# Weight splits of the second routed expert placed among the routing operations, with new planner durations for the routed blocks

## Chip, cores and metric

One core of one Trainium2 chip runs the whole program. The metric is the device time of one execution in microseconds (us); lower is better. The time before is the median of three executions.

## The reference

Three layers run one after the other: attention over a window of 64 tokens (2 batches, 8 heads, 576 tokens, head size 64), a dense mixture of 4 experts, and a routed mixture of 8 experts. 1152 tokens of 512 numbers pass through the last two. The part that matters here is the last:

```python
def _moe2_ref(x, w_skip, w_gate, w1, w2):
    do_compute = x @ w_skip > 0
    xc = x[do_compute]
    logits = xc @ w_gate
    e_idx = np.argmax(logits, axis=1)
    probs = softmax(logits); gate_w = probs[range(len(xc)), e_idx]
    for e in range(8):
        mask = e_idx == e
        h = np.maximum(xc[mask] @ w1[e], 0.0)
        y[mask] = gate_w[mask, None] * (h @ w2[e])
    out[do_compute] = xc + y
```

Each token goes to one expert or to none. w1 is 512 by 1024 and w2 is 1024 by 512 for each expert.

## The kernel before, in words

**Arithmetic.** Every fp32 operand of a large product is written as a high and a low part, and a product is three TensorE (PE) products: high by high, low by high, high by low. For weights, ScalarE (ACT) casts a loaded piece of 128 by 1024 to the high part (`hi` in `w_split`, L348), and VectorE (DVE) subtracts it to get the low part (`lo`, L351): the "split". A routed expert has two weight passes (w1 and w2, `w_pass` L1057) of four pieces each, so eight casts and eight splits. The tiles are `wa1h`, `wa1l`, `wa2h`, `wa2l` and the same with `wb`: two sets that alternate from expert to expert. Expert 0 uses wb, expert 1 wa, expert 6 wb, expert 7 wa.

**A routed block** (`block`, L948) is 128 tokens of one expert, gathered by index. First product g1 (24 PE instructions, 12 for each half of the hidden size); ACT's `hr` (relu, L989) for each half; four PE transposes `pt<-ident,hr` for each half (`turn`, L1006); ACT's and DVE's `ht` high and low (L1010, L1013); second product g2; DVE's `xg` (L1049) adds the gated result, and POOL's `scatter` (L910) writes the rows out. Within block e the tokens of block e+1 are transposed (`xpose`, L381) and split (`xsplit`, ACT L941 and DVE L943, tile `xs`), and the weights of expert e+1 are cast and split. The transposes of hr, xg, hr, xg use a ring of two PSUM buffers in turn, so the transposes of the second `hr` overwrite what DVE's first `ht` has to have read.

**Routing** (`route`, L668) runs for nine token tiles, between the last tiles of the dense layer. For each tile DVE finds the best expert (`top`, `early`) and the token's rank, PE sums into a table `tab`; `idx` (L843) makes the gather indices `idg` out of it, `num` (L853) the counts `cnt`. `gates` (L799, operations L777 to L783) splits the last two tiles' gate values in small bf16 pieces; `spread` (L785, `wy`) and PE's `tab<-wy` (L794) put them in the table, and `rest` (L867) reads them back. The first routed block takes its tokens by rank (`grab`, L760), not by index.

**What sets the order.** A small planner (`Plan`, L109) takes operations with an engine, a duration that is a formula of the size (`c_act`, `c_dve`), what they read and write, and a priority. It lists them in the order of its own simulated start, and the engines execute that static order. An operation of ACT or DVE with priority 0 or more may not start in the plan if it would delay a waiting one of negative priority by more than a margin. One plan covers the dense layer's end, routing and block 0; then there is one plan for each expert's block. After each plan but the last stands `tails` (L1175), an `If` on the counts with further blocks for experts with over 128 tokens. What an engine first has to wait for behind such an `If` it waits for as of that engine's end of the stretch before.

Of the kernel before, what the change touches and what calls it, by code (L numbers as in the profile page):

```python
# [13 lines left out]
ALU = mybir.AluOpType  # L14
# [7 lines left out]
FF = 1024  # L22
E1 = 4
E2 = 8
# [197 lines left out]

@with_exitstack
def fused_kernel(ctx: ExitStack, tc: tile.TileContext, q, k, v, dp, w1, w2, wskip, wgate, m1, m2, out):
# [116 lines left out]
    def w_split(b, ring, key, part, c, prio, pool=False, after=(), hpool=False, hdve=False):  # L341
        def aps():
            h, l = ring[f"{part}h"], ring[f"{part}l"]
            if part == 1:
                return h[:, c, :], l[:, c, :]
            return tuple(x[:, 2 * c:2 * c + 2, :].rearrange("p a n -> p (a n)") for x in (h, l))

        def hi():  # L348
            (POOL.tensor_copy if hpool else DVE.tensor_copy if hdve else ACT.copy)(out=aps()[0], in_=b.tile)  # L349

        def lo():  # L351
            h, l = aps()
            (POOL if pool else DVE).tensor_tensor(out=l, in0=b.tile, in1=f32(h), op=ALU.subtract)  # L353

        add("POOL" if hpool else "DVE" if hdve else "ACT", 3.5 if hpool else c_dve(FF // 2) if hdve else c_act(FF, False), hi, rd=[b], wr=[(key, part, "h", c)], prio=prio)
        if pool:
            add("POOL", 2.3, lo, rd=[b, (key, part, "h", c)], wr=[(key, part, "l", c)], prio=prio)
        else:
            add("DVE", c_dve(FF), lo, rd=[b, (key, part, "h", c), *after], wr=[(key, part, "l", c)], prio=prio)
        b.close()  # L360
# [307 lines left out]
    def route(t):  # L668
# [66 lines left out]
        add("DVE", 0.35, early, rd=[K("oh"), K("m8"), o0], wr=[o1, K("w0"), K("mm")], prio=P)  # L735
# [67 lines left out]
        def weigh(after):  # L803
            add("DVE", 0.8, slot, rd=[K("ps"), *after], wr=[K("r"), K("oj")], prio=1)
            if t < TT - 2:
                gates()
                spread(0, 5, 2)
            else:
                spread(0, 2, 1)
                later.append(lambda: (gates(["idg", ("htl", 4)], 15), spread(2, 5, 15, ["idg"])))  # L810
# [5 lines left out]
        if t == GT:  # L816
            add("DVE", 0.35, id0, rd=[("tab", 0), ("tab", 1)], wr=["id0"], prio=2)
# [22 lines left out]
    def route_end():  # L840
# [8 lines left out]
        add("DVE", 0.45, idx, rd=[("tab", 0), ("tab", 1)], wr=["idg"], prio=-1)  # L849
# [83 lines left out]
    def xsplit(ps, pr, n=128):  # L933

        x, w = M["xs"].buf(), KC // len(ps)
        for i, p in enumerate(ps):
# [4 lines left out]
            add("ACT", c_act(n * w), lambda v=v, hi=hi: ACT.copy(out=hi(), in_=v()), rd=[p, "M"] + ([x] if i else []),  # L941
                wr=[(x, "h", k) for k in ks], new=None if i else [x], prio=pr)
            add("DVE", c_dve(n * w), lambda v=v, hi=hi, lo=lo: DVE.tensor_tensor(out=lo(), in0=v(), in1=f32(hi()), op=ALU.subtract),  # L943
# [4 lines left out]
    def block(e, j, xg, x, small=False, amid=None):  # L948
# [29 lines left out]
        def g1(c0, w):  # L978
# [10 lines left out]
            add("ACT", c_act(128 * w), lambda: ACT.activation(out=hr[:, 0:128 * w], in_=ps[:, 0:128 * w],  # L989
# [5 lines left out]
        def tr(c0, w, hr):  # L995
# [14 lines left out]
            add("ACT", c_act(w * n), lambda: ACT.activation(out=ht[:, s, 0:n], in_=p[:, 0:w, 0:n],  # L1010
                                                            func=ACTF.Relu if small else ACTF.Copy),
                rd=[p], wr=[(ht, "h", c0)], new=[ht] if c0 == 0 else None, prio=-1)
            add("DVE", c_dve(w * n), lambda: DVE.scalar_tensor_tensor(  # L1013
# [42 lines left out]

    def w_pass(kd, e, p, prio=None):  # L1057
# [5 lines left out]
        for c in range(4):  # L1063
            extra = kd == "r" and e > 0 and p == 2
            st = KN["w2s"] if (kd, e, p) == ("m", 0, 2) else 2.5
            b = w_load(src, p, c, prio + st * c, extra, early=kd == "r" and e > 2 and p == 1)
            w_split(b, ring, key, p, c, prio + st * c, pool=(kd, e, p) == ("m", 0, 2) and KN["w2pool"][c],
                    after=["idg"] if kd == "r" and e == 1 else [])

    with tc.manual_schedule():  # L1070
# [138 lines left out]
        for e in range(E2):  # L1209
            if e < E2 - 2:  # L1210
# [5 lines left out]
            block(e, 0, xgs[e, 0], xts[e, 0], amid=None if e else route_gates)  # L1216
            if e == 0:
# [47 lines left out]
```

## Time and profile before

| | |
|---|---|
| median of 3 executions | 644.83 us (644.16 to 646.07) |
| profiled execution | 646.72 us, of which the span from first to last instruction is 644.8 us |
| PE busy | 623.1 us, 97% of the span |
| DVE, ACT, POOL busy | 52%, 36%, 12% |
| mean DMA rate | 114 GB/s |
| dense layer and routing end, block 0 begins | 482.93 us |
| blocks 1, 2, 3, 4, 5, 6, 7 begin | 498.89, 525.66, 549.21, 562.57, 598.21, 611.46, 625.30 us |
| last DVE operation and last scatter | about 639.7 and 639.98 us |

Experts 1, 2 and 4 had further blocks within their `tails`; behind experts 0, 3, 5 and 6 the next full block follows at once. Times in a timeline are microseconds from the start of the span. A time in brackets behind a row is how long the engine had been idle before it, and after the arrow what ended that wait. A letter q behind an engine's name is its sequencer, which runs the branches.

### The profile page before, as it was taken

To read this page: it belongs to the slowest core of one execution; us is meant where nothing else is said; L and a number is where in the kernel's file an instruction comes from. 1 tells how busy PE (TensorE), PEld (TensorE's weight loads), DVE (VectorE), ACT (ScalarE), POOL (GpSimd) and SP (SyncE) were. 2 spreads that over 40 slices of the span, in tenths; PEclk is the share of its full clock that TensorE was granted. 3 is DMA by queue.
4 is the path that set the end of the run, shared out by engine and by line. 5 is a ranking of instruction groups with operands and counts; after the bars stand their busy time and mean duration, and the time that the engine had idled before them with its cause. 6 is when DMAs were issued, how large, how long until landed. Compare 5 with 4: busy or idle time off the path is not lost. (4 is left out here: it accounts for less than half of the span.)

```text
span 644.8 us, 9918 instructions
## 1 busy us (share of the span) xinstructions
PE 623.1 (97%) x3742; PEld 545.3 (85%) x3742; DVE 338.5 (52%) x757; ACT 230.6 (36%) x484; POOL 76.2 (12%) x103
## 2 busy tenths in 40 slices
PE   8799999999999999999999999999998999999986
PEld 7688898998989899898989898979886778788865
DVE  5888731226612115421213526888868846872881
ACT  5668730114401113310103320202344654762761
POOL 3222320000000000000000000000104422330320
PEclk9999999999999999999999999999999999999998
DMA  9893119934700002500000511015277968692630
GB/s 222 196 286 101 35 2 2 7 12 149 243 1 0 2 1 82 179 0 1 1 0 3 197 63 72 28 66 164 80 247 236 332 214 320 214 376 76 208 132 10
DMA packets 60512, 73.49 MB, mean 114 GB/s; under 512 B 37105, under 2 KB 37105, under 8 KB 60440
## 3 DMA queue, kind: packets, MB, share of 16 engines
q1 hardware_dynamic: 57736, 64.55, 37.2%
q0 software_dynamic: 2704, 8.02, 4.0%
q8 instruction: 41, 0.67, 0.5%
q14 instruction: 31, 0.25, 0.2%
HBM read 65.85 MB, written 7.49 MB: 114 GB/s over the span
## 5 line engine op out<-in xcount | busy, mean ns | idle before, releaser
L542 PE MATMUL mm<-xth,wa1h 128*128 128x384 f32 (+1 forms) x416 | 136.9, 329 | 0.0
L542 PE MATMUL mm<-xtl,wa1h 128*128 128x384 f32 (+1 forms) x416 | 135.7, 326 | 0.0
L542 PE MATMUL mm<-xth,wa1l 128*128 128x384 f32 (+1 forms) x416 | 135.7, 326 | 0.0
L548 ACT ACTIVATE hh<-mm 128x384 fp32r<-128x384 f32 (+1 forms) x104 | 48.5, 466 | 239.6 <-PE mm L542 234.0
L563 PE MATMUL mm<-wa2h,hh 128*128 128x512 f32 (+1 forms) x296 | 117.0, 395 | 0.0
L550 DVE SCALAR_TENSOR_TENSOR hl<-mm,hh 128x384 fp32r<-128x384 f32 (+1 forms) x104 | 54.8, 527 | 117.9 <-ACT hh L548 117.3
L563 PE MATMUL mm<-wa2h,hl 128*128 128x512 f32 (+1 forms) x296 | 115.0, 389 | 0.0
L563 PE MATMUL mm<-wa2l,hh 128*128 128x512 f32 (+1 forms) x296 | 114.9, 388 | 0.0
L542 PEld LDWEIGHTS mm<-xth,wa1h 128*128 128x128 f32 x416 | 78.7, 189 | 0.7 <-issue 0.2
L542 PEld LDWEIGHTS mm<-xtl,wa1h 128*128 128x128 f32 x416 | 78.7, 189 | 0.5
L542 PEld LDWEIGHTS mm<-xth,wa1l 128*128 128x128 f32 x416 | 78.8, 189 | 0.0
L563 PEld LDWEIGHTS mm<-wa2h,hl 128*128 128x128 f32 x296 | 55.7, 188 | 12.4
L563 PEld LDWEIGHTS mm<-wa2h,hh 128*128 128x128 f32 x296 | 55.8, 188 | 11.4
L563 PEld LDWEIGHTS mm<-wa2l,hh 128*128 128x128 f32 x296 | 55.8, 188 | 11.2
L575 DVE SCALAR_TENSOR_TENSOR x<-mm,prob,x 128x512 f32<-128x512 f32 (+1 forms) x28 | 20.5, 732 | 76.2 <-PE mm L563 75.9
L818 POOL DMA_INDIRECT x<-scr,id x1 | 2.0, 1970 | 370.5 <-DMA scr<-x 370.5
L353 DVE TENSOR_TENSOR wa2l<-raw,wa2h 128x1024 fp32r<-128x1024 f32 x32 | 39.1, 1233 | 5.0 <-ACT wa2h L349 4.9
L349 ACT CAST wa2h<-raw 128x1024 fp32r<-128x1024 f32 x32 | 33.3, 1050 | 23.1 <-PE mm L563 18.6
L353 DVE TENSOR_TENSOR wa1l<-raw,wa1h 128x1024 fp32r<-128x1024 f32 x32 | 38.2, 1228 | 4.8 <-PE mm L965 3.0
L349 ACT CAST wa1h<-raw 128x1024 fp32r<-128x1024 f32 x32 | 32.0, 1046 | 16.8 <-DMA raw<-in_moe_w_dram 8.3
L1013 DVE SCALAR_TENSOR_TENSOR ht<-pt,ht 128x512 fp32r<-128x512 f32 (+2 forms) x27 | 15.1, 568 | 29.8 <-ACT ht L1010 27.5
L463 POOL TENSOR_TENSOR s<-s,mx 128x512 f32<-128x512 f32 x18 | 18.8, 1048 | 57.8 <-DVE mx L460 39.7
(212 smaller groups left out, 896.1 us busy)
## 6 DMA issues: line engine op xcount, KB each, us to landing
raw<-in_moe_w_dram SPq DMA_DIRECT2D x96, 512.0 KB
scr<-x SPq DMA_DIRECT2D x9, 256.0 KB
out_dram<-x SPq DMA_DIRECT2D x9, 256.0 KB
qn<-in_q_dram SPq DMA_DIRECT2D x8, 256.0 KB
kn<-in_k_dram SPq DMA_DIRECT2D x8, 256.0 KB
vn<-in_v_dram SPq DMA_DIRECT2D x8, 256.0 KB
raw<-wgt SPq DMA_DIRECT2D x4, 512.0 KB
qn<-in_q_dram SPq DMA_DIRECT2D x2, 128.0 KB
```

The source lines that it names most:

```text
L349: (POOL.tensor_copy if hpool else DVE.tensor_copy if hdve else ACT.copy)(out=aps()[0], in_=b.tile)
L353: (POOL if pool else DVE).tensor_tensor(out=l, in0=b.tile, in1=f32(h), op=ALU.subtract)
L463: add("POOL", 1.0, lambda: POOL.tensor_tensor(out=s.tile, in0=s.tile, in1=mx[:, 3].unsqueeze(2).to_broadcast([128, HP, 128]), op=ALU.mult) ...
L542: PE.matmul(out=ps[:, 0:n], lhsT=wa[a][:, kk, f * 128:(f + 1) * 128], rhs=x[:, kk, g0:g0 + n], start=(i == 0), stop=(i == 3 * KC - 1))
L548: add("ACT", c_act(n), lambda: ACT.activation(out=hh[:, f, 0:n], in_=ps[:, 0:n], func=ACTF.Relu), rd=[ps], wr=[("hh", f)], prio=-1)
L550: add("DVE", c_dve(n), lambda: DVE.scalar_tensor_tensor(out=hl[:, f, 0:n], in0=ps[:, 0:n], scalar=0.0, in1=f32(hh[:, f, 0:n]), op0=ALU.max ...
L563: PE.matmul(out=ps[:, 0:c1 - c0], lhsT=x[:, f, o:o + 128], rhs=wa[a][:, f, c0:c1], start=(f == 0 and i == 0), stop=(f == FC - 1 and i == 2))
L575: DVE.scalar_tensor_tensor(out=z, in0=y, scalar=prob[:, t, e:e + 1], in1=z, op0=ALU.mult, op1=ALU.add)
L818: add("POOL", 1.0, lambda: POOL.indirect_dma_start(out=R["x0"], out_offset=None, in_=scr[0:128 * (GT + 1), :], in_offset=bass.IndirectOffs ...
L1013: add("DVE", c_dve(w * n), lambda: DVE.scalar_tensor_tensor(out=ht[:, s, n:2 * n], in0=p[:, 0:w, 0:n], scalar=0.0, in1=f32(ht[:, s, 0:n]), ...
```

## The change

There are five edits. (1) `r_act` and `r_dve` are the old duration formulas plus 0.1 and 0.08 us; the planner now uses them for `hr`, `ht`, `xs` and for the casts and splits of all routed weights. (2) The four w1 splits of expert 1 no longer wait for `idg` all together. `first_lows` gives the first piece a dependence on the routing step `early` of tile 6; the second and third piece are cut in two halves of 512 columns, which depend on the last but one tile's rank matmul, on `cnt` (two of them) and on `idg`; the fourth depends on `idg`. (3) `gates` no longer depends on the low part of block 0's second `ht`. (4) `id0`, the indices of the first gather, has priority -1 in place of 2, and `idx` counts 0.7 in place of 0.45. (5) The gather for expert 0's third block is declared behind block 0 instead of ahead of it. DVE has two instructions more, since two splits became four halves.

```diff
--- before.py
+++ after.py
@@ -220,6 +220,14 @@
 
+def r_act(n, psum=True):
+    return c_act(n, psum) + 0.1
+
+
+def r_dve(n):
+    return c_dve(n) + 0.08
+
+
 @with_exitstack
@@ -338,7 +346,7 @@
 
-    def w_split(b, ring, key, part, c, prio, pool=False, after=(), hpool=False, hdve=False):
+    def w_split(b, ring, key, part, c, prio, pool=False, after=(), hpool=False, hdve=False, ca=c_act, cd=c_dve, lows=None):
         def aps():
@@ -348,15 +356,17 @@
 
-        def lo():
+        def lo(s=slice(0, FF)):
             h, l = aps()
-            (POOL if pool else DVE).tensor_tensor(out=l, in0=b.tile, in1=f32(h), op=ALU.subtract)
-
-        add("POOL" if hpool else "DVE" if hdve else "ACT", 3.5 if hpool else c_dve(FF // 2) if hdve else c_act(FF, False), hi, rd=[b], wr=[(key, part, "h", c)], prio=prio)
+            (POOL if pool else DVE).tensor_tensor(out=l[:, s], in0=b.tile[:, s], in1=f32(h)[:, s], op=ALU.subtract)
+
+        add("POOL" if hpool else "DVE" if hdve else "ACT", 3.5 if hpool else c_dve(FF // 2) if hdve else ca(FF, False), hi, rd=[b], wr=[(key, part, "h", c)], prio=prio)
         if pool:
...
         else:
-            add("DVE", c_dve(FF), lo, rd=[b, (key, part, "h", c), *after], wr=[(key, part, "l", c)], prio=prio)
+            for s, w in lows or ((slice(0, FF), after),):
+                add("DVE", cd(s.stop - s.start), lambda s=s: lo(s), rd=[b, (key, part, "h", c), *w],
+                    wr=[(key, part, "l", c)], prio=prio)
         b.close()
@@ -732,7 +742,7 @@
 
-        add("DVE", 0.35, early, rd=[K("oh"), K("m8"), o0], wr=[o1, K("w0"), K("mm")], prio=P)
+        add("DVE", 0.35, early, rd=[K("oh"), K("m8"), o0], wr=[o1, K("w0"), K("mm"), ("early", t)], prio=P)
         add("ACT", 0.24, lambda: ACT.activation(out=T("ex"), in_=src()[:, 0:E2], func=ACTF.Exp,
@@ -807,14 +817,14 @@
                 spread(0, 2, 1)
-                later.append(lambda: (gates(["idg", ("htl", 4)], 15), spread(2, 5, 15, ["idg"])))
+                later.append(lambda: (gates(["idg"], 15), spread(2, 5, 15, ["idg"])))
 
...
         if t == GT:
-            add("DVE", 0.35, id0, rd=[("tab", 0), ("tab", 1)], wr=["id0"], prio=2)
+            add("DVE", 0.35, id0, rd=[("tab", 0), ("tab", 1)], wr=["id0"], prio=-1)
             add("POOL", 1.0, lambda: POOL.indirect_dma_start(
@@ -846,7 +856,7 @@
 
-        add("DVE", 0.45, idx, rd=[("tab", 0), ("tab", 1)], wr=["idg"], prio=-1)
+        add("DVE", 0.7, idx, rd=[("tab", 0), ("tab", 1)], wr=["idg"], prio=-1)
         add("PE", 0.03, lambda: PE.matmul(out=R["pf"][:, 0:E2], lhsT=R["ones"], rhs=R[o], start=True, stop=True),
@@ -938,9 +948,9 @@
             lo = lambda i=i: x[:, i * w:(i + 1) * w, 0:n, 1]
-            add("ACT", c_act(n * w), lambda v=v, hi=hi: ACT.copy(out=hi(), in_=v()), rd=[p, "M"] + ([x] if i else []),
+            add("ACT", r_act(n * w), lambda v=v, hi=hi: ACT.copy(out=hi(), in_=v()), rd=[p, "M"] + ([x] if i else []),
                 wr=[(x, "h", k) for k in ks], new=None if i else [x], prio=pr)
-            add("DVE", c_dve(n * w), lambda v=v, hi=hi, lo=lo: DVE.tensor_tensor(out=lo(), in0=v(), in1=f32(hi()), op=ALU.subtract),
+            add("DVE", r_dve(n * w), lambda v=v, hi=hi, lo=lo: DVE.tensor_tensor(out=lo(), in0=v(), in1=f32(hi()), op=ALU.subtract),
                 rd=[p, x] + [(x, "h", k) for k in ks], wr=[(x, "l", k) for k in ks], prio=pr)
@@ -986,7 +996,7 @@
             gemm(f"g1{c0}", ps, 1, parts)
-            add("ACT", c_act(128 * w), lambda: ACT.activation(out=hr[:, 0:128 * w], in_=ps[:, 0:128 * w],
+            add("ACT", r_act(128 * w), lambda: ACT.activation(out=hr[:, 0:128 * w], in_=ps[:, 0:128 * w],
                                                               func=ACTF.Copy if small else ACTF.Relu),
@@ -1007,10 +1017,10 @@
             hr.close()
-            add("ACT", c_act(w * n), lambda: ACT.activation(out=ht[:, s, 0:n], in_=p[:, 0:w, 0:n],
+            add("ACT", r_act(w * n), lambda: ACT.activation(out=ht[:, s, 0:n], in_=p[:, 0:w, 0:n],
                                                             func=ACTF.Relu if small else ACTF.Copy),
                 rd=[p], wr=[(ht, "h", c0)], new=[ht] if c0 == 0 else None, prio=-1)
-            add("DVE", c_dve(w * n), lambda: DVE.scalar_tensor_tensor(
+            add("DVE", r_dve(w * n), lambda: DVE.scalar_tensor_tensor(
                 out=ht[:, s, n:2 * n], in0=p[:, 0:w, 0:n], scalar=0.0, in1=f32(ht[:, s, 0:n]), op0=ALU.max,
@@ -1054,6 +1064,11 @@
 
+    first_lows = [[(slice(0, FF), [("early", TT - 3)])],
+                  [(slice(0, FF // 2), [("r", "ps", (TT - 2) % 2)]), (slice(FF // 2, FF), ["cnt"])],
+                  [(slice(0, FF // 2), ["cnt"]), (slice(FF // 2, FF), ["idg"])],
+                  [(slice(0, FF), ["idg"])]]
+
     def w_pass(kd, e, p, prio=None):
@@ -1065,7 +1080,9 @@
             w_split(b, ring, key, p, c, prio + st * c, pool=(kd, e, p) == ("m", 0, 2) and KN["w2pool"][c],
-                    after=["idg"] if kd == "r" and e == 1 else [])
+                    after=["idg"] if kd == "r" and e == 1 else [],
+                    lows=first_lows[c] if (kd, e, p) == ("r", 1, 1) else None,
+                    **(dict(ca=r_act, cd=r_dve) if kd == "r" else {}))
 
@@ -1207,13 +1224,15 @@
         for e in range(E2):
-            if e < E2 - 2:
+            if 0 < e < E2 - 2:
                 xgs[e, 2] = gather(e, 2, 7, [("g2", 0)])
...
             block(e, 0, xgs[e, 0], xts[e, 0], amid=None if e else route_gates)
+            if e == 0:
+                xgs[e, 2] = gather(e, 2, 7, [("g2", 0)])
             if e == 0:
```

**DVE, block 0,** from the indices to the second half of the block as it was. `ht` is the low part of a half of the hidden layer, `wa1l` and `wa2l` are expert 1's splits.

```order
L847 TENSOR_SCALAR idg<-a 128x72
L353 TENSOR_TENSOR wa1l<-raw,wa1h 128x1024
L1013 SCALAR_TENSOR_TENSOR ht<-pt,ht 128x4x128
L353 TENSOR_TENSOR wa1l<-raw,wa1h 128x1024 x2
L1013 SCALAR_TENSOR_TENSOR ht<-pt,ht 128x4x128
L353 TENSOR_TENSOR wa1l<-raw,wa1h 128x1024
L777 TENSOR_SCALAR sc_1361<-sc_1361 128x1
...
L789 TENSOR_TENSOR wy_1356<-w_1354,oj_1350 128x216
L353 TENSOR_TENSOR wa2l<-raw_4238,wa2h 128x1024
L353 TENSOR_TENSOR wa2l<-raw_4254,wa2h 128x1024
L943 TENSOR_TENSOR xs_4417<-pt,xs_4417 128x512
```

DVE at the same place in the change:

```order
L361 TENSOR_TENSOR wa1l<-raw,wa1h 128x512 x2
L855 TENSOR_SCALAR tb<-tab 128x9x8
...
L857 TENSOR_SCALAR idg<-a 128x72
L1023 SCALAR_TENSOR_TENSOR ht<-pt,ht 128x4x128
L787 TENSOR_SCALAR sc_1361<-sc_1361 128x1
...
L799 TENSOR_TENSOR wy_1356<-w_1354,oj_1350 128x216
L1023 SCALAR_TENSOR_TENSOR ht<-pt,ht 128x4x128
L361 TENSOR_TENSOR wa1l<-raw,wa1h 128x512
L361 TENSOR_TENSOR wa1l<-raw,wa1h 128x1024
L953 TENSOR_TENSOR xs_4415<-pt,xs_4415 128x512
```

The first `wa1l` and three of the four halves are now ahead of `idg` (two halves are the fence's first row); only a half and a whole are left behind it. They stand behind `wy` and the second `ht`, and the gates follow the first `ht` directly. All four `wa2l` come behind the block's `xg` (before: two ahead of it, two behind).

**DVE, block 6,** whose weights are expert 7's, as it was; a first `wa1l` stands ahead of the two shown. The blocks 2 to 5 show the same pattern.

```order
L353 TENSOR_TENSOR wa1l<-raw,wa1h 128x1024 x2
L1013 SCALAR_TENSOR_TENSOR ht<-pt,ht 128x4x128
L353 TENSOR_TENSOR wa1l<-raw,wa1h 128x1024
L353 TENSOR_TENSOR wa2l<-raw_7318,wa2h 128x1024
L943 TENSOR_TENSOR xs_7397<-pt,xs_7397 128x512
L1013 SCALAR_TENSOR_TENSOR ht<-pt,ht 128x4x128
L353 TENSOR_TENSOR wa2l<-raw_7327,wa2h 128x1024
L943 TENSOR_TENSOR xs_7422<-pt,xs_7422 128x512
L353 TENSOR_TENSOR wa2l<-raw_7352,wa2h 128x1024
L1049 SCALAR_TENSOR_TENSOR xg<-mm,gates,xg 128x512
L353 TENSOR_TENSOR wa2l<-raw_7367,wa2h 128x1024
L1177 COMPARE_AND_BRANCH
```

DVE in block 6 in the change, again behind a first `wa1l`:

```order
L361 TENSOR_TENSOR wa1l<-raw,wa1h 128x1024 x2
L1023 SCALAR_TENSOR_TENSOR ht<-pt,ht 128x4x128
L953 TENSOR_TENSOR xs_7395<-pt,xs_7395 128x512
L1023 SCALAR_TENSOR_TENSOR ht<-pt,ht 128x4x128
L361 TENSOR_TENSOR wa1l<-raw,wa1h 128x1024
L953 TENSOR_TENSOR xs_7419<-pt,xs_7419 128x512
L361 TENSOR_TENSOR wa2l<-raw_7320,wa2h 128x1024
L1059 SCALAR_TENSOR_TENSOR xg<-mm,gates,xg 128x512
L361 TENSOR_TENSOR wa2l<-raw_7329,wa2h 128x1024
L361 TENSOR_TENSOR wa2l<-raw_7353,wa2h 128x1024
L361 TENSOR_TENSOR wa2l<-raw_7362,wa2h 128x1024
L1194 COMPARE_AND_BRANCH
```

Both list all eight splits of the next expert. Before, seven stand ahead of `xg` and one behind it. After, five stand ahead and three behind.

**PE, block 5,** around the transposes of the first half of the hidden layer, as it was; blocks 1 to 6 show the same.

```order
L965 MATMUL mm<-wa1h,xs_6440 128x512
L965 MATMUL mm<-wa1l,xs_6440 128x512
L1006 MATMUL pt<-ident,hr 128x128 x4
L965 MATMUL mm<-wa1h,xs_6440 128x512
L965 MATMUL mm<-wa1l,xs_6440 128x512
L965 MATMUL mm<-wa1h,xs_6440 128x512
L965 MATMUL mm<-wa1l,xs_6440 128x512
L965 MATMUL mm<-wa1h,xs_6440 128x512 x4
L965 MATMUL mm<-wa2h,ht 128x512
```

PE at the same place in the change:

```order
L975 MATMUL mm<-wa1h,xs_6437 128x512
L975 MATMUL mm<-wa1l,xs_6437 128x512
L975 MATMUL mm<-wa1h,xs_6437 128x512
L975 MATMUL mm<-wa1l,xs_6437 128x512
L975 MATMUL mm<-wa1h,xs_6437 128x512
L975 MATMUL mm<-wa1l,xs_6437 128x512
L1016 MATMUL pt<-ident,hr 128x128 x4
L975 MATMUL mm<-wa1h,xs_6437 128x512 x4
L975 MATMUL mm<-wa2h,ht 128x512
```

The transposes `pt<-ident,hr` stand behind 20 of the 24 g1 instructions, not behind 16, so that four instead of eight lie between them and the first g2 instruction, which reads `ht`.

## Rows read from the trace of the kernel before

**Rows 1.** The page's busy time: us, share of the span, instructions.

```profile
PE 623.1 (97%) x3742; PEld 545.3 (85%) x3742; DVE 338.5 (52%) x757; ACT 230.6 (36%) x484; POOL 76.2 (12%) x103
```

**Rows 2.** PE's waits from 440 to 645: us in total, times, longest.

```profile
PE mm L965 <- DVEq L1177: 1.9, 1, 1.9
PE tab L794 <- DVE gb L780: 1.5, 1, 1.5
```

**Rows 3.** DVE's timeline, block 0 and start of block 1: start, us, operation.

```profile
486.70 0.20 DVE L847 TENSOR_SCALAR idg<-a 128x72 uint32<-128x72 f32 x1
486.81 1.22 DVE L353 TENSOR_TENSOR wa1l<-raw,wa1h 128x1024 fp32r<-128x1024 f32 x1
488.95 0.69 DVE L1013 SCALAR_TENSOR_TENSOR ht<-pt,ht 128x512 fp32r<-128x512 f32 x1 [0.92 <-ACT ht L1010]
489.56 2.35 DVE L353 TENSOR_TENSOR wa1l<-raw,wa1h 128x1024 fp32r<-128x1024 f32 x2
...
495.90 0.67 DVE L789 TENSOR_TENSOR wy<-w,oj 128x216 bf16<-128x216 bf16 x2
...
501.19 2.35 DVE L353 TENSOR_TENSOR wa2l<-raw,wa2h 128x1024 fp32r<-128x1024 f32 x2
```

**Rows 4.** PE's timeline of the same stretch, with its waits.

```profile
490.10 0.33 PE L1006 MATMUL pt<-ident,hr 128*128 128x128 f32 x1 [0.69 <-ACT hr L989]
...
496.33 0.55 PE L794 MATMUL tab<-wy,r 128*128 128x216 bf16 x2 [1.46 <-DVE gb L780]
...
499.22 0.40 PE L965 MATMUL mm<-wa1l,xs 128*128 128x512 f32 x1
499.45 0.39 PE L965 MATMUL mm<-wa1h,xs 128*128 128x512 f32 x1
...
503.75 0.63 PE L1006 MATMUL pt<-ident,hr 128*128 128x128 f32 x4 [0.89 <-DVEq L1177]
```

**Rows 5.** PE's timeline, end of block 2.

```profile
536.02 0.66 PE L381 MATMUL pt<-ident,xg 128*128 128x128 f32 x4 [0.28 <-DVE xs L943]
```

**Rows 6.** DVE's timeline, end of block 5 and block 6.

```profile
611.35 0.75 DVE L1049 SCALAR_TENSOR_TENSOR xg<-mm,gates,xg 128x512 f32<-128x512 f32 x1
612.02 1.22 DVE L353 TENSOR_TENSOR wb2l<-raw,wb2h 128x1024 fp32r<-128x1024 f32 x1
613.49 3.50 DVE L353 TENSOR_TENSOR wa1l<-raw,wa1h 128x1024 fp32r<-128x1024 f32 x3 [0.26 <-ACT wa1h L349]
616.90 0.68 DVE L1013 SCALAR_TENSOR_TENSOR ht<-pt,ht 128x512 fp32r<-128x512 f32 x1
...
624.65 0.75 DVE L1049 SCALAR_TENSOR_TENSOR xg<-mm,gates,xg 128x512 f32<-128x512 f32 x1
625.32 1.22 DVE L353 TENSOR_TENSOR wa2l<-raw,wa2h 128x1024 fp32r<-128x1024 f32 x1
```

**Rows 7.** PE's timeline, block 6 and start of block 7.

```profile
615.26 0.64 PE L1006 MATMUL pt<-ident,hr 128*128 128x128 f32 x4
...
618.96 0.60 PE L1006 MATMUL pt<-ident,hr 128*128 128x128 f32 x4
...
625.30 0.47 PE L965 MATMUL mm<-wa1h,xs 128*128 128x512 f32 x1 [0.69 <-PEq L1177]
627.69 0.50 PE L965 MATMUL mm<-wa1l,xs 128*128 128x512 f32 x1 [1.92 <-DVEq L1177]
```

**Rows 8.** The same of block 4's second transposes, and DVE's xg ahead of that block.

```profile
562.46 0.75 DVE L1049 SCALAR_TENSOR_TENSOR xg<-mm,gates,xg 128x512 f32<-128x512 f32 x1
...
570.07 0.60 PE L1006 MATMUL pt<-ident,hr 128*128 128x128 f32 x4
```

**Rows 9.** ACT's timeline in block 6.

```profile
616.02 0.60 ACT L1010 ACTIVATE ht<-pt 128x512 fp32r<-128x512 f32 x1
```

**Rows 10.** Windows: stretch, length, five engines' busy us, granted clock, DMA share, GB/s.

```profile
629.60:631.60 2.00, 2.00 (x10) 1.90 (x9) 0.00 (x0) 0.60 (x1) 0.00 (x0) 0.50 0.00 0
```

## The prediction

> **What bounds the kernel now.** I read the page's busy times first. PE is busy 623.1 of 644.8 us [rows 1], so a gain can only come from the 22 us in which PE waits or runs slowly, and any new gap of PE is paid in full. Next I read PE's waits from the first routing steps to the end [rows 2]. The reader is to see that two waits on DVE alone make 3.4 us. Then I took DVE's and PE's timelines of the stretches in which these waits lie.
>
> In block 0, PE stands still three times in a way that this change can touch: 0.69 us at the transposes of the second `hr`, 1.46 us at `tab<-wy`, and, already in block 1, 0.89 us at the first transposes [rows 4]. The last one sets the time of all the others. Block 1 stands behind an `If`, and its first transposes wait for DVE's last two splits of the stretch before, which end at 501.19 + 2.35 = 503.54; the transposes start at 503.75, 0.21 later [rows 3, 4]. A shorter wait earlier in block 0 moves nothing as long as DVE's end stays: DVE is the bound there. From `ht` on (488.95) DVE has no gap up to that end, 14.59 us of work.
>
> The second place is block 7. Its second matmul waits 1.92 us, again for DVE's end of the stretch before: the last split ends at 625.32 + 1.22 = 626.54, and the matmul starts at 627.69, 1.15 later [rows 6, 7].
>
> **Block 0 and the start of block 1: -3.5 us.** A split in a run of two takes 1.13 us (2.35 less 1.22, [rows 3]). Before, four wa1l splits stand behind `idg`; one fills the time up to `ht`, three come behind it. In the change a whole one and a half are left. For the half I take 0.60: `ht`, which has its 512 columns, takes 0.69 alone and the next row starts 0.61 after it [rows 3]. So behind `ht` DVE's work falls by 3 x 1.13 - 1.13 - 0.60 = 1.66 us. `ht` itself can come earlier, since block 0's first half starts earlier on PE: behind the last rank operation PE has fewer gather matmuls left, about 0.9 us. It stood at 488.95 with 0.92 us idle ahead of it, so the transposes and ACT set it, and DVE's split of 1.22 did not. I take 487.95, giving 1.0 us. DVE's end moves from 503.54 to about 500.9, and PE's restart from 503.75 to 501.1: -2.6. On top, in the change 20 g1 matmuls stand ahead of these transposes, 16 before; the four run while PE waits, at 0.23 each [rows 4]: -0.9. The two other gaps of block 0 (0.69 and 1.46) go as well, because eight g2 matmuls now stand ahead of the second transposes and the gates follow the first `ht` at once; that is what lets PE reach block 1 before DVE's end, and they are not added again. Bounds: -2.6 if `ht` stays where it was, and -4.4 if DVE's end were out of the way and PE alone counted (0.69 + 1.46 + 0.89 + 0.9, and some tenths for restarts).
>
> The halves are two instructions more. By the rows, two of them take 1.20 against 1.13, 0.07 us each pair; three of the four lie ahead of `idg`, where DVE waits for PE. [...]
>
> **The end of block 2: -0.4 us.** PE waits 0.28 us there for DVE's `xs` [rows 5], and the first matmul behind a gap takes about 0.1 longer. In the change `xs` follows the first `ht` directly, with two splits less ahead of it. Bounds -0.5 and 0.
>
> **Blocks 4 and 6: +0.9 us each.** Two splits move from ahead of `xg` to behind it, so DVE enters the next block with three to do. In block 6: `xg` ends at 612.02, three splits take 3.4, the gap 0.1 to 0.26, three `wa1l` 3.4, and `ht` 0.68 [rows 6]: `ht` ends at 619.6 to 619.9 where it ended at 617.6. Its cover is PE's work up to 618.96, when the second transposes want to overwrite what `ht` reads [rows 7]. With 0.06 to 0.2 for the hand-over, PE starts them at 619.8, 0.9 late. In block 4 the same sum starts at 563.13 and gives 570.7 to 571.0 against 570.07 [rows 8]: +0.9. Bounds 0.6 and 1.1. Blocks 2 and 5 don't pay this: the blocks in the `tails` ahead of them need no splits, so DVE has time to catch up. Block 3 likewise.
>
> **Block 7: +2.3 us beyond block 6's 0.9.** PE waits for DVE's end, and that end now has three splits behind `xg` instead of one: 2 x 1.13 = 2.3. This cover is gone because nothing but one matmul stands ahead of the waiting one on PE. The second matmul goes from 627.69 to about 630.9. Bounds: 1.3, if the 0.94 us by which this hand-over is longer than block 1's runs beside DVE's splits, and 2.3.
>
> **The transposes four matmuls later, blocks 1 to 6: +0.6 us.** From the start of the transposes to the first g2 matmul there are now 0.38 + 4 x 0.23 + about 0.1 = 1.4 us. ACT's `ht` starts 0.76 behind the transposes' start and takes 0.60: 1.36 [rows 7, 9], and then PE has to learn of it. I take 0.1 per block, bounds 0 and 0.2. Block 0 has eight transposes' worth of other work there and pays nothing.
>
> **Small blocks, three of them (behind experts 2 and 4, and block 7): +0.6 us.** Their transposes also move four matmuls back; these have half the columns, so about 0.12 each. The cover for ACT's `ht` shrinks by 0.5. I take 0.2 each, bounds 0 and 0.5.
>
> **Edits that I cost at nothing.** The higher priority of `id0` moves 0.7 us of small DVE operations behind routing work in a part where the splits had filled DVE; its gather feeds later work, with 10 us and more to spare. The gather of expert 0's third block is a declaration inside an `If` that isn't taken. On SP a weight load passes one store, on POOL the count loads pass a gather; what they feed is wanted microseconds later. If that cover were gone, each would cost a few tenths.
>
> **The sum** is -3.5 - 0.4 + 0.9 + 0.9 + 2.3 + 0.6 + 0.6 = +1.4 us. Made against the profiled execution it gives 646.72 + 1.4 = 648.1. That execution is 1.9 above the median of the three, so on the median it is 646.2. Its own range, by the bounds that matter, is 645.0 to 647.6.
>
> **Rivals.** What a measurement can tell from no change is 0.3%, 1.9 us: below 642.9 is faster, above 646.8 slower.
>
> *The hand-overs have slack (faster).* In block 7 PE resumes 1.15 behind DVE's last split, in block 1 only 0.21. If the difference is PE's own branching, counted from 625.30, it runs beside DVE's two further splits: -1.0. If the `ht` hand-over also fits and the small blocks lose nothing, -1.2 more, and with the first gain nearer its upper bound (-0.9) the sum is -1.7 to -2.2: about 642.9. Against it: the branches stand behind the split on DVE itself, so that they come after it.
>
> [...]
>
> *The splits move, but block 1 doesn't.* If the small routing operations between the halves push `idg` back by what the halves take ahead of it, DVE's end moves 1.6 instead of 2.6, and the sum is +2.4: 647.2.
>
> **How the numbers follow.** Forecast 0.50; since it ends 0.6 below the line to slower, 0.34 of that is same and 0.16 slower. Slack 0.25: 0.18 faster, 0.07 same. Clock 0.18, slower. Block 1 unmoved 0.07: 0.03 same, 0.04 slower. Together faster 0.18, same 0.44, slower 0.38. The range goes from 642.6, which leaves out the lower part of the slack case, to 648.2, which leaves out the clock case with the other upper bounds.
>
> **What would show it.** Right: no wait of PE at `tab<-wy` and at block 0's second transposes; block 1's first transposes near 501.1; a wait of about 0.9 at the second transposes of blocks 4 and 6, for DVE's `ht`; block 7's wait near 4 us, and three `wa2l` splits ahead of it. Wrong: block 7's wait unchanged or block 1's restart still near 503; short new waits for ACT's `ht` at the first g2 matmul absent in blocks 1 to 6, or longer than 0.2; and above all PE gaps at places that I have not named.

## The result and the profile after

| | before | after |
|---|---|---|
| median of 9 executions each, same comparison | 646.07 us (644.16 to 648.46) | 649.90 us (648.18 to 659.95) |
| ratio, 95% interval | | 1.0058 [1.0038, 1.0078], slower by 3.75 us |
| profiled execution, its span | 646.72, 644.8 us | 650.85, 649.1 us |
| block 0 begins; from there to block 2 | 482.93; 42.73 us | 480.42; 44.86 us |
| block 2 to block 3 | 23.55 us | 23.14 us |
| block 3 to the end | 95.59 us | 100.68 us |

The forecast was 646.2 (642.6 to 648.2), the same within 0.3% as the likeliest. The time lies above the range. 1.2 of the 3.7 us between them is the median of before, which rose from 644.83 to 646.07 with six more executions; the rest is the change, +3.75 where +1.4 was forecast. PE's busy time, beside [rows 1], did not grow while the span grew by 4.3 us, so the time went into waits; what the clock adds is read from the windows below:

```profile
PE 622.2 (96%) x3742; PEld 543.6 (84%) x3742; DVE 338.2 (52%) x759; ACT 232.1 (36%) x484; POOL 75.5 (12%) x103
```

PE's waits of the changed kernel, from 440 us to the end (us in total, times, longest), beside [rows 2]:

```profile
PE mm L975 <- DVEq L1194: 3.0, 1, 3.0
PE pt L1016 <- DVEq L1194: 2.3, 1, 2.3
PE mm L975 <- ACTq L1194: 2.2, 1, 2.2
PE pt L1016 <- DVE ht L1023: 1.7, 2, 0.9
```

The wait at `tab<-wy` (1.46) is gone, as forecast. In its place PE waits twice in block 1: 2.2 for ACT and 2.3 for DVE. The 1.7 is two waits of 0.86 in blocks 4 and 6, and the 3.0 is block 7's. These are the four longest; one of 0.67 in block 0, which the forecast did not name, comes up at the count loads. PE's timeline at these places, beside [rows 4, 7]:

```profile
480.42 0.51 PE L975 MATMUL mm<-wb1h,xs 128*128 128x512 f32 x1 [0.47 <-ACT xs L951]
...
492.09 0.63 PE L391 MATMUL pt<-ident,xg 128*128 128x128 f32 x4
...
496.96 0.51 PE L975 MATMUL mm<-wa1h,xs 128*128 128x512 f32 x1 [2.19 <-ACTq L1194]
...
504.20 0.63 PE L1016 MATMUL pt<-ident,hr 128*128 128x128 f32 x4 [2.33 <-DVEq L1194]
...
570.36 0.63 PE L1016 MATMUL pt<-ident,hr 128*128 128x128 f32 x4 [0.86 <-DVE ht L1023]
...
620.54 0.63 PE L1016 MATMUL pt<-ident,hr 128*128 128x128 f32 x4 [0.86 <-DVE ht L1023]
...
627.08 0.47 PE L975 MATMUL mm<-wa1h,xs 128*128 128x512 f32 x1 [0.85 <-DVE xg L1059]
630.53 0.79 PE L975 MATMUL mm<-wa1l,xs 128*128 128x512 f32 x1 [2.99 <-DVEq L1194]
```

From block 0's start to the transposes at 504.20 it takes 23.78 us; before it was 503.75 - 482.93 = 20.82 [rows 4], the forecast was 19.07. DVE's timeline of that stretch and of block 6, beside [rows 3, 6]:

```profile
483.00 1.27 DVE L361 TENSOR_TENSOR wa1l<-raw,wa1h 128x512 fp32r<-128x512 f32 x2
...
485.19 0.20 DVE L857 TENSOR_SCALAR idg<-a 128x72 uint32<-128x72 f32 x1
487.45 0.69 DVE L1023 SCALAR_TENSOR_TENSOR ht<-pt,ht 128x512 fp32r<-128x512 f32 x1 [2.06 <-ACT wa2h L357]
...
491.42 1.82 DVE L361 TENSOR_TENSOR wa1l<-raw,wa1h 128x512 fp32r<-128x512 f32 x2
496.94 0.69 DVE L953 TENSOR_TENSOR xs<-pt,xs 128x512 fp32r<-128x512 f32 x1 [3.70 <-ACTq L1194]
...
499.38 4.62 DVE L361 TENSOR_TENSOR wa2l<-raw,wa2h 128x1024 fp32r<-128x1024 f32 x4
...
616.30 3.50 DVE L361 TENSOR_TENSOR wa1l<-raw,wa1h 128x1024 fp32r<-128x1024 f32 x3 [0.26 <-DVEq L1194]
619.71 0.68 DVE L1023 SCALAR_TENSOR_TENSOR ht<-pt,ht 128x512 fp32r<-128x512 f32 x1
...
626.94 3.49 DVE L361 TENSOR_TENSOR wa2l<-raw,wa2h 128x1024 fp32r<-128x1024 f32 x3
```

Two idle times are new. DVE is idle for 2.06 us between `idg` and the first `ht`, where before a split ran [rows 3], and for 3.70 ahead of `xs`. What it waits for ahead of `xs` is ACT's part of `xs`, a cast:

```profile
496.30 0.61 ACT L951 CAST xs<-pt 128x512 fp32r<-128x512 f32 x1 [4.58 <-remote]
```

PE's transposes that this cast reads began at 492.09 and take 0.63. ACT starts the cast 3.6 us behind the end that PE's rows give them; what it waits for until then is taken up in the experiments. In the trace of before the cast started 0.63 behind the transposes' start (494.90 against 494.27), and DVE had two `wa2l` splits to do ahead of its own `xs`. Now all four `wa2l` stand behind `xs`, so the cast's lateness is passed on to DVE's end (499.38 + 4.62 = 504.00) and 0.20 later to PE.

The first idle time is explained by DVE's sequencer. A view of one source line (engine, count: shortest, median, longest ns, first and last start) shows the three loads of the counts that the `If`s read; the first line is of after, the second of before:

```profile
L1134 DVEq TENSOR_LOAD <-cnt x3: 308/314/548, 485.8 to 486.8; - x3
```

```profile
L1117 DVEq TENSOR_LOAD <-cnt x3: 308/314/548, 487.3 to 488.3; - x3
```

Before, a split of 1.22 us was started between `idg` and the loads, at 486.81 [rows 3], and about half of the loads ran beside it. After, no split stands there, and the loads are in the open. PE has three such loads of its own, from 485.0 to 486.0, and stood still for 0.67 us up to 486.68; before, it had no such wait. DVE's end, not this, decides when block 1's transposes start.

Windows of the end (stretch, length, busy us of the five engines, granted clock, DMA share, GB/s), beside [rows 10]:

```profile
631.00:632.00 1.00, 1.00 (x4) 0.71 (x4) 0.00 (x0) 0.00 (x0) 0.00 (x0) 0.50 0.07 16
...
635.00:636.00 1.00, 1.00 (x6) 1.00 (x6) 0.00 (x0) 0.30 (x1) 0.00 (x0) 0.50 0.00 0
636.00:637.00 1.00, 1.00 (x10) 1.00 (x8) 0.00 (x0) 0.08 (x1) 0.00 (x0) 0.79 0.00 0
```

The granted clock fell to 0.50 at about 629.6, while PE waited (0.80 in the window from 629 to 630). PE's work from block 7's second matmul at 630.53 to about 636.4 ran at this clock, 5.9 us. The kernel before left and came back to the full clock in the next two windows, so it was low for some 3.4 us:

```profile
628.00:629.00 1.00, 1.00 (x5) 0.84 (x4) 0.00 (x0) 0.00 (x0) 0.00 (x0) 0.85 0.69 238
...
632.00:633.00 1.00, 1.00 (x11) 1.00 (x10) 0.00 (x0) 0.39 (x2) 0.00 (x0) 0.94 0.00 0
```

From block 7's second matmul to the end of the span there are 18.57 us, where there were 17.11.

### The profile page after: what moved, and what is told of

It reads as the page before. It is cut to its first block, busy times and chain, and to the rows that moved or that the text cites. A ratio compares the mean times of both kernels' runs of the same rounds, so it can differ in the third digit from the quotient of the medians.

```text
span 649.1 us, 9931 instructions
## 1 busy us (share of the span) xinstructions
PE 622.2 (96%) x3742; PEld 543.6 (84%) x3742; DVE 338.2 (52%) x759; ACT 232.1 (36%) x484; POOL 75.5 (12%) x103
## 5 line engine op out<-in xcount | busy, mean ns | idle before, releaser
L361 DVE TENSOR_TENSOR wa1l<-raw,wa1h 128x1024 fp32r<-128x1024 f32 (+1 forms) x34 | 38.1, 1155 | 5.1 <-PE mm L975 2.8
L1023 DVE SCALAR_TENSOR_TENSOR ht<-pt,ht 128x512 fp32r<-128x512 f32 (+2 forms) x27 | 15.1, 569 | 25.7 <-ACT ht L1020 22.3
L921 POOL DMA_INDIRECT out_dram<-xg,ids x11 | 16.0, 1459 | 84.0 <-DVE xg L1059 65.2
```

Of the source, the lines that this page charges most:

```text
L361: (POOL if pool else DVE).tensor_tensor(out=l[:, s], in0=b.tile[:, s], in1=f32(h)[:, s], op=ALU.subtract)
L921: add("POOL", 1.0, lambda: POOL.indirect_dma_start(out=out, out_offset=bass.IndirectOffsetOnAxis(ap=R["ids"][0:n, j, e:e + 1], axis=0), in ...
L1023: add("DVE", r_dve(w * n), lambda: DVE.scalar_tensor_tensor(out=ht[:, s, n:2 * n], in0=p[:, 0:w, 0:n], scalar=0.0, in1=f32(ht[:, s, 0:n]), ...
```

## The experiments

All edits are made to the changed kernel, unless it says otherwise. `EXTRA` is a factor on the 0.1 and 0.08 us that `r_act` and `r_dve` add.

**Which half costs?** The first kernel keeps the change's plan of the dense end, routing and block 0, and plans all later blocks with the old durations. The second is the reverse: edits 2 to 5 undone, and the new durations only from expert 1's plan on.

```diff
 def r_act(n, psum=True):
-    return c_act(n, psum) + 0.1
+    return c_act(n, psum) + 0.1 * EXTRA[0]
...
             if e == 0:
+                EXTRA[0] = 0.0
                 route_ps.close()
```

> The order of the first plan (dense layer's end, routing, block 0) as in the change, every later block in the order of before. Theory (the loss sits in the later blocks' splits behind xg): PE's two waits of 0.86 us in blocks 4 and 6 are gone, block 7's second matmul waits about 1.9 us instead of 2.99, and the clock is at 0.50 for some 4 us instead of 6; 1.7 + 1.1 + 1.5 less, 0.4 given back in block 2: about 4 us faster than the change, 0.998 to 1.002 of before. Rival (the loss sits in block 0, where ACT's xs comes at 496.30 after 4.58 us of idling): the later waits vanish but the ratio stays above 1.003.

> The first plan in the order of before, every later block in the order of the change. Theory: waits for DVE's ht of 0.9 us in blocks 4 and 6, block 7's wait near 3 us or longer and the clock at 0.50 for 6 us: 3.5 to 4.5 us slower than before, ratio 1.0055 to 1.007. Rival (the loss sits in block 0): within 1.5 us of before, ratio under 1.0025.

Measured: the first part alone 647.46 us, ratio 1.0016 [0.9999, 1.0034]; the later part alone 649.17, 1.0043 [1.0027, 1.0060]. The two add up to the change's 1.0058. So the later blocks lose 2.8 us, and the first plan, which was to give a gain, gives none. The second kernel's trace has the 0.86 and 0.85 at blocks 4 and 6 and the 2.99 at block 7, as the whole change has. The first kernel's has ACT's wait again, here it begins 2.24 us behind the transposes' start (494.68). ACT's idle time of 3.05 is not all lateness; it was 2.49 before, where the cast began 0.63 behind them.

```profile
496.92 0.61 ACT L954 CAST xs<-pt 128x512 fp32r<-128x512 f32 x1 [3.05 <-PE tab L807]
```

**What holds ACT?** A hint on the coming branch is placed on four engines inside block 0. In two kernels ACT has none (the second also has the first part only), which tests whether ACT's idle time comes from its own hint.

```diff
-            tc.mark_branch_hint_location(f"more{e}", hint=further(e), engines=[x.engine for x in (PE, ACT, DVE, POOL)])
+            tc.mark_branch_hint_location(f"more{e}", hint=further(e), engines=[x.engine for x in ((PE, ACT, DVE, POOL) if e else (PE, DVE, POOL))])
```

> The change, with the branch hint of block 0's If taken away for ACT alone. [...] Rival (ACT waits for data): ACT's xs stays near 16 us behind the start of block 0, ratio 1.005 to 1.007. Third: ACT's hint matters but the branch then stands late in its place, and ACT idles behind the If instead.

> Both of the edits: the first plan of the change without ACT's hint at block 0, later blocks as before. [...] Rival (ACT waits for data, not for instructions): the same as the first plan of the change alone, 0.998 to 1.002.

Measured: 649.69, 1.0054 [1.0034, 1.0074], and 645.85, 1.0010 [0.9992, 1.0028]. ACT's idle time ahead of `xs` is 3.06 in both traces, and the cast is late in both, so ACT's own hint is not the cause.

Next, three tiny copies that wait for nothing stand on ACT ahead of block 1's `xs`: if they run at once, the data hold the cast, and if they are late as well, the stream itself stands still. In the other kernel 40 such copies stand in the dense layer, which puts ACT's later instructions 40 places further on in its stream.

```diff
+    def look():
+        for i in range(3):
+            ACT.copy(out=tiny[:, i:i + 1], in_=ident[:, i:i + 1])
```

> The change with three tiny ACT copies, which wait for nothing, directly ahead of block 1's xs, behind the last wa2h cast. If ACT waits for data (the transposes, or a count on PE that comes late), the three run within 0.5 us of the cast's end and the gap stands behind them, between the third and xs. If ACT itself can't go on (its instructions aren't there yet), the gap of 3 to 4.6 us stands ahead of the first, or between two of the three.

> The change with 40 tiny ACT copies spread over the dense layer, one behind each of 40 hh, so that every later ACT instruction stands 40 further on in its stream and in the memory that it is fetched from. If the gap ahead of block 1's xs belongs to a place in the instruction stream (a fetch), it goes there: xs within 0.8 us of the transposes of xg, block 1's first transposes 2 to 3.5 us earlier against block 0's start, ratio to before 1.001 to 1.003. If ACT waits for data, xs stays 2.2 to 4.2 us behind the transposes and the ratio stays at 1.005 to 1.007.

Measured: 648.07 in its only execution; and 648.50, 1.0072 [1.0045, 1.0100], of four. Both are inconclusive, because neither trace has the gap, ACT's long idle time ahead of a late cast. In the first, the cast begins 0.63 behind the transposes at 493.88:

```profile
494.51 0.63 ACT L960 CAST xs<-pt 128x512 fp32r<-128x512 f32 x1 [0.53 <-PE pt L392]
```

From block 0's start to block 1's transposes it is 20.04 and 20.06 us in these two traces, against 23.78 in the change's.

**What does the clock cost?** PE multiplies the identity by itself some times at the end of block 6, ahead of block 7's wait: 11 times in the change, 7 times in the kernel before, and 7 times in the first part alone. The results are not used.

```diff
+            def fill():
+                for _ in range(11):
+                    PE.matmul(out=wb.tile[:, 0, :], lhsT=ident, rhs=ident, start=True, stop=True)
+
+            add("PE", 0.1, fill, rd=["ident", ("g2", np_ - 1)], new=[wb], prio=2000)
```

> The change with 11 matmuls of the identity at the end of block 6, behind its last g2 matmul, which write a spare PSUM buffer: they fill some 2.4 us of the 4 us in which PE stands still there. If the low clock of block 7 (0.50 for 6 us) comes from that standstill, it is at 1.00 from the second matmul on or soon after, block 7 from there to its end takes some 3 us less, and the ratio to before goes from 1.0058 to 1.001 to 1.0025. If the clock falls all the same, nothing changes (1.005 to 1.007). Block 7's second matmul stays where it is, at DVE's end.

> The kernel before with 7 matmuls of the identity at the end of block 6. If block 7's slow clock (0.50 to 0.85 for 4 us) comes from PE's standstill ahead of it, the clock is at 1.00 there and the time falls by 1.5 to 2 us: ratio 0.997 to 0.998. Rival: the clock falls all the same, ratio 1.

> The first plan of the change, the later blocks of before, and the 7 matmuls. Theory: first_part_only's 1.0016 less 1.5 to 2 us: 0.9985 to 0.9993, the same as before within 0.3%.

Measured: in the change 646.27, 1.0015 [0.9998, 1.0032]; in the kernel before 644.61, 0.9975 [0.9954, 0.9995]; in the first part 643.61, 0.9976 [0.9952, 0.9999]. The clock stays at 1.00 in block 7. First the change with the copies, then before with them:

```profile
629.00:630.00 1.00, 1.00 (x5) 0.82 (x5) 0.00 (x0) 0.00 (x0) 0.00 (x0) 1.00 0.03 8
...
631.00:632.00 1.00, 1.00 (x11) 1.00 (x10) 0.00 (x0) 0.65 (x2) 0.00 (x0) 1.00 0.00 0
```

```profile
630.00:631.00 1.00, 1.00 (x11) 0.99 (x9) 0.00 (x0) 0.45 (x2) 0.00 (x0) 1.00 0.00 0
```

From block 7's second matmul to the end it is now 15.73 us in the kernel before and 15.99 in the change, against 17.11 and 18.57 without the fillers. So the low clock cost 1.4 us before and costs 2.6 in the change; of the 1.46 by which this stretch grew, 1.2 is the clock. In the kernel before the timing agrees: 0.25% of 645 is 1.6 us. In the change, from 1.0058 (or 1.0048, repeated below) to 1.0015 it is 2.1 to 2.8, but this does not confirm the 2.6: the trace with the copies has no gap in block 0, while both traces of the change have one, so the two prices are not separated in the timing.

The trace of the change with the copies has the change's order on ACT, and no gap:

```profile
494.52 0.63 ACT L951 CAST xs<-pt 128x512 fp32r<-128x512 f32 x1 [0.79 <-PE pt L391]
```

There block 1's transposes come 20.02 us behind block 0's start, and block 2 starts 41.10 behind it, where before it was 42.73.

**Are the count loads DVE's idle time?** The loads' latest place in the plan moves from 1.5 to 8 us, in the change and in the first part with fillers.

```diff
-                add("X", 0.0, counts, rd=["cnt"], wr=["nv"], slack=1.5)
+                add("X", 0.0, counts, rd=["cnt"], wr=["nv"], slack=8.0)
```

> The change with the count loads let in 8.0 instead of 1.5 later in the plan: DVE's three loads of cnt stand behind the last wa1l split instead of directly ahead of block 0's first ht, and POOL's stand behind the gathers instead of ahead of them. Theory: in the change the loads hold DVE's first ht back by 1.1 us against what was forecast (7.03 us behind block 0's start instead of 5.9), because the split that lay beside them before has moved; here ht comes at about 5.9 and block 1's first transposes at 19.0 instead of 20.0 behind block 0's start (where ACT's gap does not come in), 1 us faster than the change. Since the gathers also start earlier, PE's transposes of xg find their rows landed, and if ACT's gap hangs on that it does not come. Rival (the loads only wait there because ht's own input is late): ht stays at 7.0.

> first_fill with the late count loads as well. Theory (loads 1 us, clock 1.5 to 2 us, ACT's gap of 2 to 4 us gone if the gathers' start sets it): 3 to 5 us under first_part_only, ratio 0.993 to 0.997, faster than both kernels. Rival (the gap is still there in most executions): 0.997 to 0.999.

Measured: 652.88, 1.0104 [1.0069, 1.0140], and 648.08, 1.0036 [1.0018, 1.0053]. `ht` does come earlier: 5.31 us behind block 0's start (480.48) instead of 7.03, held now by ACT's `ht`. DVE's row, and PE's of the same kernel:

```profile
485.79 0.69 DVE L1023 SCALAR_TENSOR_TENSOR ht<-pt,ht 128x512 fp32r<-128x512 f32 x1 [0.34 <-ACT ht L1020]
```

```profile
494.18 0.29 PE L804 MATMUL tab<-wy,r 128*128 128x216 bf16 x1 [1.69 <-DVE xs L953]
...
500.59 0.48 PE L975 MATMUL mm<-wa1h,xs 128*128 128x512 f32 x1 [2.71 <-PEq L1194]
```

So the loads hold `ht` by 1.7 us, together with the branch hint, which reads the counts and moved along with them; in the kernels of the next experiment that have the loads and no hint, `ht` stands at 6.75, so the hint's share is 0.28. But moving them costs more than it gives: PE enters block 1 20.1 us behind block 0's start, where the change's own trace has 16.5. On PE the hint now comes some 0.25 us ahead of the `If`, and the branch itself takes 6.09 us where it takes 0.48 in the change (count: shortest, median, longest ns; first of the change, then of this kernel):

```profile
L1194 PEldq COMPARE_BRANCH  x1: 475/475/475, 492.3 to 492.3; - x1
```

```profile
L1194 PEldq COMPARE_BRANCH  x1: 6090/6090/6090, 494.3 to 494.3; - x1
```

**Does the gap belong to the order?** The change and the first part were run once more, and the first part with fillers too, unchanged, on another chip; and the hint of block 0 was taken off all four engines, in the kernel before, in the first part and in the first part with fillers.

```diff
             else:
-                add("PE", 0.05, lambda: hint(e), rd=["nv", ("g10", 1)], wr=[("g10", 2)], prio=10.0)
+                return
```

> The change once more, for a second trace of it. If ACT's gap ahead of block 1's xs belongs to this program or this order, it is there again (xs 2 us or more behind the transposes of xg); if it comes and goes with the execution, it may be gone, and block 1's first transposes then stand 20.0 us behind block 0's start, as in the traces without the gap. Ratio to before 1.003 to 1.007 in either case.

> first_part_only once more. With the gap, 22.3 us from block 0's start to block 1's first transposes and a ratio near 1.0016; without it 20.0 us and 0.998.

> first_fill once more, beside the next one on the same chip: ratio 0.995 to 1.000; 20.0 us from block 0's start to block 1's first transposes if ACT's gap is not there, 22.3 if it is.

> first_part_only without the branch hint of block 0's If on any engine. [...]

> The kernel before without the branch hint of block 0's If. Control for first_no_hint: if the hint costs something only in the change's block 0 (where it comes while ACT and PE are ahead of DVE), the ratio is 0.999 to 1.003; if it costs every kernel, 0.996 to 0.998.

> The first plan of the change, the later blocks of before, 7 matmuls at the end of block 6, and no branch hint at block 0's If. [...] Rival (first_no_hint's 0.9972 was the executions, not the hint): the same as first_fill_b within its interval.

| kernel | median us | ratio, 95% interval |
|---|---|---|
| the change again | 648.85 | 1.0048 [1.0028, 1.0067] |
| first part again | 647.40 | 1.0011 [0.9984, 1.0037] |
| first part with fillers, again | 645.67 | 0.9986 [0.9958, 1.0013] |
| before without hint | 649.93 | 1.0057 [1.0034, 1.0079] |
| first part without hint | 644.82 | 0.9972 [0.9952, 0.9992] |
| first part with fillers, without hint | 642.95 | 0.9962 [0.9938, 0.9986] |

The gap is back in the first three; ACT is idle for 3.09, 3.11 and 3.09 us. The same kernel, the first part with fillers, has it in one trace and not in the other, and its median is 643.61 in the run without the gap and 645.67 in the one with it (before beside them: 645.26 and 645.42), though the intervals of the ratios overlap. First the trace without the gap, then the one with it:

```profile
492.27 0.63 ACT L954 CAST xs<-pt 128x512 fp32r<-128x512 f32 x1 [0.85 <-PE pt L394]
```

```profile
495.00 0.61 ACT L954 CAST xs<-pt 128x512 fp32r<-128x512 f32 x1 [3.09 <-PE mm L978]
```

The transposes that the cast reads began at 491.60 and 492.37. Block 1's transposes then come 20.07 and 22.30 behind block 0's start. So the order of the instructions alone does not decide the gap. Of the traces with a known chip, those in which the cast was late came from two chips and those without it from two others, one execution of each kernel; that is no proof that the chip decides.

Which engine is late can be read from the updates of the semaphores, which the traces also hold. The cast waits for PE's semaphore, and in all 15 traces with the new first plan that semaphore is updated 0.02 to 0.03 us ahead of the cast's start: at 494.98 in the second of the two traces above, and at 496.28 in the change's first. So ACT is not late; it starts as soon as PE reports the transposes, and the report is late against PE's rows, whose ends are modelled. In the traces with the gap the updates for the transposes and for the `tab` products behind them come 0.03 to 0.04 us apart, as if held up together; in those without it 0.09 to 0.10. PE is late for itself as well: block 1 begins 16.0 to 16.5 us behind block 0's start in the seven traces of this plan with a late cast, and 14.3 in the four without.

Without the hint, the kernel before loses 0.6%: PE itself is late behind the `If`, where its branch takes 5.64 us instead of 0.38.

```profile
503.20 0.48 PE L965 MATMUL mm<-wa1h,xs 128*128 128x512 f32 x1 [3.83 <-PEq L1177]
```

In the change's first plan the opposite holds, 0.9972 without it against 1.0011 with it, though the intervals touch and the trace that was taken (647.12) is not typical of its median. With the fillers it is 0.9962 against 0.9986, again with intervals that overlap, though the two were timed side by side and their medians are 2.7 us apart; 642.95 is the lowest median of all, below both kernels. ACT's idle time is 2.00 there, not 3.09:

```profile
494.63 0.61 ACT L954 CAST xs<-pt 128x512 fp32r<-128x512 f32 x1 [2.00 <-PE tab L807]
```

## Why the prediction was wrong

**Block 0 and the start of block 1, -3.5: this step failed.** The 0.9 in it for four g1 matmuls ahead of the transposes was right: with the old first plan and the new later ones, block 0's start to block 2's is 41.90 us, where before it was 42.73, so -0.83. The -2.6 failed, by two assumptions:

- "`ht` itself can come earlier ... I take 487.95". That is 5.9 us behind the start of block 0 that I forecast (482.93 - 0.9), and it was 7.03. I had read the idle 0.92 in [rows 3] as the transposes and ACT, and that "DVE's split of 1.22 did not" set it. The split was cover for the count loads. With it gone the loads and the hint behind them hold `ht` back, by 1.7 us as the experiment on the loads shows, 1.1 of it beyond my forecast. DVE's work from `ht` on was sized right: in an execution without a gap block 1's transposes come 20.07 us behind block 0's start, 1.0 more than the forecast's 19.07.
- "From `ht` on DVE has no gap up to that end." With two `wa2l` splits fewer ahead of `xs`, there is nothing left to do when ACT's part is late, as it is when PE's report of the transposes is. Against 0.65 us from the transposes' start to the cast's, the largest lateness was 3.6 us, in the change's first trace. Eleven traces have this first plan with the loads in place and at most ACT's hint off; in seven the cast is late, by 1.6 to 3.6, and there the restart comes 22.3 to 23.8 us behind block 0's start. In the trace of before the two splits would have covered 3.2 us: ACT's `xs` ended at 495.5, DVE began its own at 498.76. I priced the move of these splits in blocks 4, 6 and 7, and not in block 0.

The first plan alone gave 1.0016, 1.0011 and, without ACT's hint, 1.0010: +0.6 to +1.0 us, hardly to be told from nothing, instead of -2.6. How many of the timed executions had the gap is not shown, since one execution of each run was traced. What it does gain is at its start: block 0 begins 27.79 us behind the dense layer's last hidden product in the traces of the new first plan, and 28.0 to 28.8 behind it with the old one.

**The end of block 2, -0.4:** right, 23.55 became 23.14.

**Blocks 4 and 6, +0.9 each:** right, 0.86 twice, and for the stated reason: in block 6 `ht` starts at 619.71 behind three splits that were still to do. The time from block 3's start to the second block of expert 4 grew by 1.11 us, and from there to block 6's second transposes by 1.26.

**Transposes four matmuls later and small blocks, +0.6 each:** too high. What the two stretches hold beyond the waits of 0.86 is 0.25 and 0.40, so 0.65 and not 1.2. No wait of PE for ACT's `ht` shows in any block.

**Block 7, +2.3:** the mechanism was right, the size not. Three splits stand behind `xg` and PE waits for DVE's end, but from block 6's second transposes to block 7's second matmul it took 9.99 us after 8.73: +1.26, the lower bound, which I had put at 1.3 for the case that part of the hand-over runs beside the splits. The last split ends at 626.94 + 3.49 = 630.43, and PE starts 0.10 later; before it was 1.15 later [rows 6, 7]. The traces show that this difference existed, not why.

**The clock case, 0.18 in the forecast, came true on top.** My estimate of its price was 1.0 to 1.5 us, for 2 to 3 us more at the 0.50 of [rows 10]; the traces show 2.5 us more (5.9 after 3.4), and 1.2 us. I took it as the alternative to the forecast, though nothing in it excluded the other terms. The longer wait, 2.99 us after 1.92, did not shorten the slow stretch.

**Halves.** Two half splits take 1.27 us where a whole one takes 1.22 [rows 3], so 0.05 for the extra instruction; I had 0.07.

**Sum.** In the traces the part from block 2 on is -0.41 + 5.09 = +4.7 us, where the forecast had +4.9 by other terms: block 7 1.0 less, the two small terms 0.55 less, the stretch behind block 7's wait 1.46 more. Timed, the later part alone is +2.8, or +3.6 without the 0.83 of block 1, so this part was forecast a little too high. What made the forecast wrong is the first plan: a gain of 2.6 was counted on, where the timed runs show +0.6 to +1.0.

What stays open is why PE's report of the transposes, and with it ACT's cast, comes late in some executions and not in others; no run shows it. ACT's own hint is excluded. The kernels without any hint point to the hints of the other engines, but their cast is still 0.9 and 1.2 us late.

## What to carry to other kernels

When work is moved away from a place, look at what ran beside it there, on the sequencer as well: a split that set no time still covered register loads, and two splits ahead of a join would have covered most of a hand-over that is 1.6 to 3.6 us late in some executions. Price the same move at every place where it happens; here a split put behind `xg` or `xs` was costed in blocks 4, 6 and 7 and not in block 0. And where PE must wait near the end, a few spare matmuls ahead of the wait, 7 or 11 here, kept its clock at 1.00, where it was 0.50 without them, and were worth 1.6 us even in the kernel before.

## What was not expected of the hardware

- A hand-over between two engines took 2 us longer in one execution of one and the same kernel than in another: 0.67 and 2.63 us from the start of the transposes to the start of the cast that reads them. The cast followed PE's semaphore update within 0.03 us both times; the update was late.
- Three loads of a count into DVE's registers (0.31 to 0.55 us each, with the semaphores ahead of them) left the engine, with the branch hint behind them, idle for 2.06 us, more than the 1.22 of a whole split.
- The branch hint ahead of one `If` is worth 0.57% to the kernel before, some 3.7 us, and nothing or less than nothing to the new first plan (1.0011 with it and 0.9972 without, with fillers 0.9986 and 0.9962). PE's branch took 0.38 us in the kernel before and 0.48 in the change; it took 5.64 in the kernel before without the hint, and 6.09 with the count loads moved and the hint 0.25 us ahead of the `If`.
